# Weight steps of the first MLP by a list of places, and the next batch's attention spread evenly behind them

## The chip, the core and the metric

The kernel runs on one core of a Trainium2 chip. TensorE (PE) multiplies into eight banks of PSUM; VectorE (DVE), ScalarE (ACT) and GpSimd (POOL) compute beside it, and SyncE (SP) issues the DMAs. Each engine works through its own queue in order and waits on semaphores for the others. The metric is the device time of one launch in microseconds. Before the change the median of three runs is 712.6 us (712.22 to 713.0).

## The reference

Four batches of 768 steps pass through three layers, all in float32: a gated linear attention (8 heads of 48), a mixer with a channel MLP, and a gated unit.

```python
state = alpha[:, :, t, :, None] * state + np.einsum('bhd,bhe->bhde', k[:, :, t], v[:, :, t])
y[:, :, t] = np.einsum('bhd,bhde->bhe', q[:, :, t], state)
...
h = xt @ U @ V
u = x + h.transpose(0, 2, 1)
ch = np.maximum(u @ w_ch1, 0.0) @ w_ch2        # 384 -> 1536 -> 384
return (u + ch).astype(np.float32)
...
h = np.maximum(x @ w_in, 0.0)                  # then norm, spatial product, gate, w_out
```

The weights of the MLP arrive as 64-bit floats.

## The kernel before

**Float32 by halves.** A float32 operand is kept as a high part and a rest, and each product is made of three matmuls (`mm3`, `up_group`, lines 259 and 345).

**The weights.** The MLP's weights w_ch1 and w_ch2 come in twelve tiles, W0 to W11 (index `f`), each 128 by 768. Turning one tile from 64-bit words into two parts takes six instructions on three engines: `low_part` on ACT (L211), two integer operations on DVE (L217, L220), an addition on POOL (L223, which needs both), then `split` copies the sum into the high part on ACT (L564) and subtracts for the rest on DVE (L228). `Stage.begin` issues the first four; each call of `Stage.finish(1)` issues one of the last two for the oldest tile begun. So between the addition on POOL and the copy on ACT stands a semaphore: ACT waits in its queue until POOL is done.

**The first MLP.** Batch 0's attention (`first_batch`) runs ahead of everything. Then the MLP of batch 0 runs: up products of nine matmuls into one of two banks ("mm"), ACT takes the positive part (h, L360), DVE its rest (hl, L341), and two groups later nine down products add into three banks. At the end of a run of tiles DVE adds those banks to the block (L411). `FIRST` sets the runs: tiles 0 to 4 for both halves of the sequence side by side (the second half's sums lie in the banks "x" that attention uses otherwise), then runs of tiles, one half after the other.

**What is woven in.** After every three matmuls the MLP calls `pull()`. In batch 0 it begins and finishes weight tiles at the calls listed in `BEGINS` and `ENDS`, and advances batch 1's attention (`attend(1)`) by as many steps as `due()` says. `need(n)` forces a tile's conversion when a group is about to use it. Nothing else sets the order: each engine's queue is the order in which this code issues.

**Attention of batch 1.** Four pairs of heads, numbered 4 to 7. For a pair: two scans on DVE ahead of it (`prepare`, L690 and L702), each followed by a multiplication on POOL (L679); `flip` on PE, taken to SBUF by ACT as kn (L734); `added` on PE; then `state`: ACT writes the decays (L781) into spare columns of one of the two PAIR banks and copies the sums out (L782), and DVE runs six scans (L785) that read the decays there; `keep` on ACT (L795, L796); `scores` on PE into the PAIR banks and their mask on DVE (L756); `inner` and `outer` products on PE (L806, L816) and their `take` on ACT (L831). `mix` steps turn the pair before (L946, L962); they use the bank ALONE.

Of the kernel before, what the change touches and what calls it, by code (L numbers as in the profile page):

```python
# [47 lines left out]
NP = H // 2  # L48
# [4 lines left out]
DS = 8  # L53
NCH = S // CH
# [20 lines left out]
PAIR = PLACES["x"][0:2]  # L75
# [18 lines left out]
def gla_mixer_gating_kernel(ctx: ExitStack, tc: tile.TileContext, akq, v, vT, u, v3, w12, w_in, wsT, b_sp, w_out, out):  # L94
    nc = tc.nc
# [38 lines left out]
    class Stage:  # L134
# [4 lines left out]
        def __init__(self, pool, items, places=(), width=E, most=1):  # L139
            self.narrow = lambda: pool.tile([128, width], U32, name="narrow", tag="narrow", bufs=2)  # L140
            self.items, self.free = list(items), list(places)
            self.loaded, self.late, self.begun, self.most, self.scaled = [], [], 0, most, 0

        def fill(self, most=99):
            while self.items and len(self.loaded) < most:
# [24 lines left out]
            low_part(self.loaded[self.scaled][1])  # L170
            self.scaled += 1

        def begin(self, room=None):
# [6 lines left out]
            place, words, t, n, wide, finish = self.loaded.pop(0)  # L180
            if wide and not place:
                t = (room or self.narrow())[0 : words.shape[0], 0:n]
            if wide and not self.scaled:
                low_part(words)
            self.scaled = max(0, self.scaled - 1)
            x = narrowed(words, t) if wide else words
            self.late.append((self.begun, finish(x), place))
            self.begun += 1
            return True

        def step(self):
# [21 lines left out]
    def narrowed(words, t):  # L213

        words = words.rearrange("p (n w) -> p n w", w=2)
        low, high = words[:, :, 0], words[:, :, 1]
# [3 lines left out]
        nc.vector.scalar_tensor_tensor(  # L220
            out=t, in0=high, scalar=0xC0000000, in1=t, op0=ALU.bitwise_and, op1=ALU.bitwise_or
        )
        nc.gpsimd.tensor_tensor(out=t, in0=t, in1=low, op=ALU.add)  # L223
        return t.bitcast(F32)

# [83 lines left out]
    class ChannelMlp:  # L309
# [54 lines left out]
        def up_both(self, blocks, f):  # L364
            w = self.wts
            wh, wl = w[f][:, 0], w[f][:, 1]
            both = [self.psp.tile([128, 512], F32, name="ps_1", tag="mm") for _ in blocks]

            for ends in (False, True):
                for (t, uh, ul), ps in zip(blocks, both):  # L370
                    parts = [(wh, ul, k) for k in range(KE)] if ends else [(wx, uh, k) for wx in (wh, wl) for k in range(KE)]
                    for i, (wx, ux, k) in enumerate(parts):
                        nc.tensor.matmul(
                            out=ps[:, 0:TB], lhsT=wx[:, k * 128 : (k + 1) * 128], rhs=ux[:, k, :],
                            start=i == 0 and not ends, stop=ends and i == KE - 1,
                        )
# [203 lines left out]
    with ExitStack() as fast:  # L580
# [133 lines left out]
        class Pair:  # L714
# [61 lines left out]

            def state(self, pd):

                decay = pd[:, 0, TB : TB + DS * NCH]
                pe = seen[:, seq[self.n], 1:].rearrange("p (o c) -> p o c", o=1)  # L780
                nc.scalar.activation(out=decay.rearrange("p (e c) -> p e c", c=NCH), in_=pe.to_broadcast([128, DS, NCH]), func=AF.Copy)  # L781
                nc.scalar.activation(out=add.rearrange("p (n x) -> p x n", x=SIDES), in_=pd[:, :, 0 : D * NC], func=AF.Copy)  # L782
                after = apool.tile([128, D, NCH], F32, name="after", tag="after", bufs=1)
                for e in range(0, D, DS):
                    nc.vector.tensor_tensor_scan(  # L785
                        out=after[:, e : e + DS].rearrange("p e c -> p (e c)"), data0=add[:, e * NCH : (e + DS) * NCH], data1=decay,
                        initial=0.0, op0=ALU.add, op1=ALU.mult,
                    )
                self.after = after
# [189 lines left out]
        def attend(b, blocks):  # L979
# [5 lines left out]
            if b * NP not in ready:  # L985
# [6 lines left out]
                yield  # L992
                next(p0)
                yield
            for i in range(NP):
                n = b * NP + i
# [16 lines left out]
                move_some(moves, 3)  # L1013
                yield
                pair.mask(pair.scores())
                next(ahead, None)
                move_some(moves, 3)
                yield
                move_some(moves, 3)
# [6 lines left out]
                yield  # L1026
                if n + 3 < NPAIR:
                    load_pair(n + 3)
                mix = Mix(us, pair.hp, stk) if pair.hp < KE else None
                yield  # L1030
            mix.take(mix.flip(0))
# [37 lines left out]
        def first_batch(blocks):  # L1069
# [27 lines left out]
            for n in range(NP - 1):  # L1097
# [7 lines left out]
                pair.inner(0)  # L1105
                next(ahead)
                if n == 2:
                    weights.scale()
                    weights.scale()
# [17 lines left out]
            weights.begin(narrow[0])  # L1127
            weights.begin(narrow[1])
            weights.scale()
# [9 lines left out]
            flipped(0)  # L1139
            weights.finish(1)  # L1140
            weights.begin()
# [8 lines left out]
            weights.finish(1)  # L1150
            weights.finish(1)
            gp = mixes[0].product()
            weights.finish(1)
            mixes[0].keep(gp)
            flipped(2)
# [4 lines left out]
            summed(1, 0)  # L1160
            gp = mixes[2].product()
            mixes[2].keep(gp)
            for blk in range(NB):
# [3 lines left out]
            for m, blk, engine in (  # L1167
                (0, 0, nc.gpsimd), (0, 1, nc.gpsimd), (1, 0, nc.gpsimd), (2, 0, nc.vector), (1, 1, nc.vector), (2, 1, nc.vector)
            ):
                t, hi, lo = blocks[blk]  # L1170
                rest(lo[:, m, :], t[:, m, :], hi[:, m, :], engine)
            weights.finish(1)
            weights.finish(1)
            yield
            load_pair(5)
# [5 lines left out]
        rest_of_first = first_batch(blocks)  # L1181
        next(rest_of_first)
        nxt = []
        more = attend(1, nxt)
        steps = chain(rest_of_first, more)

        def gating_steps():
            yield from check_alpha()
# [20 lines left out]
        def pull():  # L1209

            nonlocal pulls, done
            pulls += 1
            if b == 0 and pulls in ENDS:
                weights.finish(1)
            if b == 0 and pulls in BEGINS:
                weights.begin()
# [12 lines left out]
        def need(n):  # L1229
            weights.until(N_SMALL + n)  # L1230
# [3 lines left out]
        mlp = ChannelMlp(w12s.parts, hpool, ps, pull, need)  # L1234
        for b in range(B):
            if b == 0:
                n_steps = N_STEPS + 4
# [204 lines left out]
```

## Time and profile before

| what | us |
|---|---|
| median of three runs | 712.6 |
| the profiled execution | 714.88 |
| its span | 712.9 |
| PE busy | 685.0 |
| DVE busy | 342.3 |
| ACT busy | 283.7 |
| POOL busy | 203.1 |

The profiled execution took 714.88 us, of which 712.9 lie between its first and last instruction. Busy times are unions of an engine's instructions; PE's ends are modelled, so its busy time says little about its pace. What an engine waited for, and when, is read from the timeline.

### The profile page before, as it was taken

What the parts mean: (1) busy time and instruction counts of PE and PEld (TensorE: products, weight loads), DVE (VectorE), ACT (ScalarE), POOL (GpSimd) and SP (SyncE); (2) the same over time, 40 slices, a digit from 0 to 9 for tenths busy, and PEclk for the clock granted to TensorE, in tenths of its full rate; (3) what the DMA queues carried; (4) which work ended last, traced back from release to release, by engine and by line L of the source; (5) the groups of instructions that cost most, each with busy time, mean ns of one, the idle gap of its engine ahead of it and who ended that gap; (6) DMA issues with size and microseconds to landing.
All of it is one profiled execution on the core that took longest, in us unless ns stands there. A gap on an engine that the chain in (4) does not pass through costs nothing.

```text
span 712.9 us, 14466 instructions
## 1 busy us (share of the span) xinstructions
PE 685.0 (96%) x6124; PEld 653.9 (92%) x6124; DVE 342.3 (48%) x620; ACT 283.7 (40%) x552; POOL 203.1 (28%) x172
## 2 busy tenths in 40 slices
PE   7988878999999999999999999999999999999996
PEld 6878867899999999999999999989999989999996
DVE  7998987556444335433132784351252143225211
ACT  3874446664454534454331543332231232224111
POOL 5534533215111031110030131343333223333211
PEclk9999999999999999999999999999999999999999
DMA  8699104443543310401004353300011003000001
GB/s 335 194 346 225 28 2 85 78 92 69 114 72 68 81 22 8 111 2 35 2 1 158 103 165 107 122 1 31 5 35 65 34 1 100 9 26 24 11 34 39
DMA packets 21178, 54.20 MB, mean 76 GB/s; under 512 B 2704, under 2 KB 12816, under 8 KB 19824
## 3 DMA queue, kind: packets, MB, share of 16 engines
q1 hardware_dynamic: 21104, 53.18, 27.5%
q8 instruction: 50, 0.82, 0.5%
q14 instruction: 24, 0.20, 0.1%
HBM read 42.55 MB, written 9.44 MB: 73 GB/s over the span
## 4 chain that ended last, share of the span: by engine, by line
PE 82%; DVE 12%; ACT 3%; issue 2%; POOL 1%; DMA 0%; DVEq 0%; ACTq 0%
PE banks L353 19%; PE banks L262 18%; PE banks L264 17%; PE banks L263 17%; PE banks L816 2%; DVE bw L690 2%; DVE narrow L217 1%; DVE fw L702 1%; PE banks L962 1%; PE banks L747 1%; PE banks L806 1%; DVE w L228 1%; PE banks L774 1%; PE banks L731 1%; PE banks L946 1%
## 5 line engine op out<-in xcount | busy, mean ns | idle before, releaser
L353 PE MATMUL banks<-partuh,w 128*128 128x384 f32 x564 | 131.0, 340 | 4.6 <-DVE hl L341 4.6
L353 PEld LDWEIGHTS banks<-partuh,w 128*128 128x128 f32 x564 | 100.4, 189 | 6.2 <-DVE hl L341 5.8
L341 DVE SCALAR_TENSOR_TENSOR hl<-banks,h 128x384 fp32r<-128x384 f32 x96 | 52.9, 552 | 104.0 <-ACT h L360 103.3
L262 PE MATMUL banks<-h,w 128*128 128x384 f32 x288 | 99.9, 347 | 0.9 <-DVE ub L411 0.9
L264 PE MATMUL banks<-hl,w 128*128 128x384 f32 x288 | 96.9, 336 | 0.0
L263 PE MATMUL banks<-h,w 128*128 128x384 f32 x288 | 96.7, 336 | 0.0
L513 DVE TENSOR_TENSOR vsb<-banks,bb 128x384 f32<-128x384 f32 x32 | 17.8, 558 | 129.2 <-PE banks L264 129.2
L360 ACT ACTIVATE h<-banks 128x384 fp32r<-128x384 f32 x94 | 45.8, 488 | 73.8 <-PE banks L353 73.2
L228 POOL TENSOR_TENSOR partul<-ub,partuh 128x384 fp32r<-128x384 f32 x45 | 46.1, 1049 | 88.7 <-ACT partuh L297 75.9
L519 ACT ACTIVATE gh<-gt 128x384 fp32r<-128x384 f32 x32 | 16.8, 525 | 126.3 <-DVE gt L516 126.3
L228 POOL TENSOR_TENSOR gl<-gt,gh 128x384 fp32r<-128x384 f32 x32 | 32.5, 1015 | 120.7 <-ACT gh L519 120.7
L263 PE MATMUL banks<-wsph,vl 128*128 128x384 f32 x192 | 65.1, 339 | 1.0 <-POOL vl L228 0.9
L353 PE MATMUL banks<-partul,w 128*128 128x384 f32 x282 | 66.0, 341 | 0.0
L262 PE MATMUL banks<-wsph,vh 128*128 128x384 f32 x192 | 64.9, 338 | 0.0
L264 PE MATMUL banks<-wspl,vh 128*128 128x384 f32 x192 | 64.8, 338 | 0.0
L262 PEld LDWEIGHTS banks<-h,w 128*128 128x128 f32 x288 | 54.4, 189 | 2.7 <-DVE ub L411 1.6
L263 PEld LDWEIGHTS banks<-h,w 128*128 128x128 f32 x288 | 54.5, 189 | 0.0
L264 PEld LDWEIGHTS banks<-hl,w 128*128 128x128 f32 x288 | 54.4, 189 | 0.0
L353 PEld LDWEIGHTS banks<-partul,w 128*128 128x128 f32 x282 | 50.0, 189 | 0.7
L679 POOL TENSOR_TENSOR akq<-akq,bw 128x768 f32<-128x768 f32 (+1 forms) x15 | 24.6, 1640 | 82.4 <-DVE bw L690 82.4
L679 POOL TENSOR_TENSOR akq<-akq,fw 128x768 f32<-128x768 f32 (+1 forms) x15 | 24.9, 1662 | 62.6 <-DVE fw L702 50.9
L228 POOL TENSOR_TENSOR vl<-vt,vh 128x512 fp32r<-128x512 f32 x20 | 27.1, 1379 | 49.8 <-ACT vh L483 49.8
(184 smaller groups left out, 1374.0 us busy)
## 6 DMA issues: line engine op xcount, KB each, us to landing
akq<-in_akq SPq DMA_DIRECT2D x24, 434.4 KB, 7.3
bits<-in_w SPq DMA_DIRECT2D x12, 768.0 KB, 13.3
x2d<-ub SPq DMA_DIRECT2D x8, 576.0 KB, 3.4
ub<-x2d SPq DMA_DIRECT2D x8, 576.0 KB, 5.3
out_y<-ob SPq DMA_DIRECT2D x24, 192.0 KB, 1.9
v<-in_v SPq DMA_DIRECT2D x15, 288.0 KB, 7.7
words<-in_w_in SPq DMA_DIRECT2D x8, 384.0 KB, 3.2
words<-in_wsT SPq DMA_DIRECT2D x4, 576.0 KB, 5.2
```

The lines of the kernel that those rows point to most:

```text
L228: engine.tensor_tensor(out=out, in0=x, in1=hi.bitcast(F32), op=ALU.subtract)
L262: nc.tensor.matmul(out=ps, lhsT=wh, rhs=xh, start=first, stop=False)
L263: nc.tensor.matmul(out=ps, lhsT=wl, rhs=xh, start=False, stop=False)
L264: nc.tensor.matmul(out=ps, lhsT=wh, rhs=xl, start=False, stop=last)
L341: nc.vector.scalar_tensor_tensor(out=hl, in0=ps[:, 0:TB], scalar=0.0, in1=h.bitcast(F32), op0=ALU.max, op1=ALU.subtract)
L353: nc.tensor.matmul(out=ps[:, 0:TB], lhsT=wx[:, k * 128 : (k + 1) * 128], rhs=ux[:, k, :], start=i == 0, stop=i == len(parts) - 1)
L360: nc.scalar.activation(out=h, in_=ps[:, 0:TB], func=AF.Relu)
L513: nc.vector.tensor_tensor(out=vsb, in0=psv[:, 0:TB], in1=self.g["bb"][:, blk * TB : (blk + 1) * TB], op=ALU.add)
L519: nc.scalar.activation(out=hi, in_=gt, func=AF.Copy)
L679: engine.tensor_tensor(out=chunks(x)[:, c], in0=chunks(x)[:, c], in1=chunks(by)[:, c, 1:CW], op=ALU.mult)
L690: nc.vector.tensor_tensor_scan(out=bw[:, ::-1], data0=a[:, 1 : AW + 1][:, ::-1], data1=ends[:, ::-1], initial=0.0, op0=ALU.mult, op1=ALU.max)
L816: nc.tensor.matmul(out=self.py[HW * h : HW * h + D, x, j * CH : (j + 1) * CH], lhsT=self.w[:, c - 1, h, :], rhs=self.q[:, c * CH : (c + 1) ...
```

## The change

`FIRST` gets one more run: tiles 8 and 9, then 10 and 11, each one half after the other, in place of 8 to 11. One list, `FIRST_STEPS`, says at which `pull()` a tile is finished by one step ("f"), begun ("b"), or attention advances by one step ("s"). Attention is otherwise spread evenly from pull 71. `up_both` calls `pull()` once more, so later calls bear a number higher by one. `begin` is cut in `high` and `add`, and the DVE operations now stand ahead of `low_part` on ACT. In `state` the decays go to the bank ALONE, and `mix.flip(1, ALONE)` stands ahead of them. The last part of `prepare` (a check on ACT, L706) moves to the end of a pair. In `first_batch` two of four copies move from DVE to ACT, and two of three rests from POOL to DVE.

```diff
-FIRST = (0, 5, 8, 12)
+FIRST = (0, 5, 8, 10, 12)
-BEGINS = (1, 9, 17, 25, 34, 43, 54, 65, 76, 87)
-AHEAD, N_AHEAD, HELD = 20, 5, 62
-ENDS = tuple(x + y for x in BEGINS for y in (10, 12))
+FIRST_STEPS = {
+    5: "f", 6: "b", 13: "fbf", 22: "fbf", 31: "fbf", 40: "fbf", 49: "fbf", 58: "f", 59: "ss", 67: "ss",
+    76: "fbf", 86: "fbf", 98: "fbf", 110: "fbf", 116: "f", 122: "f",
+}
+AHEAD, N_AHEAD = 71, 4
...
+        def high(self, room=None):
+            place, words, t, n, wide, finish = self.loaded.pop(0)
...
+            self.raised.append((place, words, t, wide, finish, self.scaled > 0))
+            self.scaled = max(0, self.scaled - 1)
+        def add(self):
+            place, words, t, wide, finish, scaled = self.raised.pop(0)
+            if wide and not scaled:
+                low_part(words)
+            x = both_parts(words, t) if wide else words
+            self.late.append((self.begun, finish(x), place))
...
                 hs.append((h, hl))
+                if len(hs) == 1:
+                    self.pull()
...
-                decay = pd[:, 0, TB : TB + DS * NCH]
+                decay = ps.banks[:, ALONE, TB : TB + DS * NCH]
...
+                if mix:
+                    pt = mix.flip(1, ALONE)
                 pair.state(pair.added())
                 if mix:
-                    mix.take(mix.flip(1, ALONE))
+                    mix.take(pt)
...
-            for x in range(NB):
-                pair.take(x, nc.vector)
+            pair.take(0)
+            pair.take(1, nc.vector)
...
-            if b == 0 and pulls in ENDS:
-                weights.finish(1)
-            if b == 0 and pulls in BEGINS:
-                weights.begin()
+            if b == 0:
+                for x in FIRST_STEPS.get(pulls, ""):
+                    if x == "f":
+                        weights.finish(1)
+                    elif x == "b":
+                        weights.begin()
+                    else:
+                        next(steps, None)
...
-            if mlp.held or pulls <= HELD:
-                return min(N_AHEAD, (pulls - AHEAD) // 4)
-            return N_AHEAD + -(-(pulls - HELD) * (n_steps - N_AHEAD) // (groups - HELD))
+            return -(-max(0, pulls - AHEAD) * (n_steps - N_AHEAD) // (groups - AHEAD))
```

The first place is DVE's queue where the side-by-side run ends. The tile W7 is `bits_370`, and its rest is the row `w12_913` before and `w12_924` now; `ub_177` and `ub_178` are the two halves' sums. Before:

```order
L228 TENSOR_TENSOR w12_913<-narrow_873,w12_913 128x768
L341 SCALAR_TENSOR_TENSOR hl_927<-banks_80,h_926 128x384
L411 TENSOR_TENSOR ub_177<-banks_80,ub_177 128x384 x3
L341 SCALAR_TENSOR_TENSOR hl_953<-banks_80,h_952 128x384
L411 TENSOR_TENSOR ub_178<-banks_80,ub_178 128x384 x3
L690 SCALAR_TENSOR_TENSOR bw_123<-akq1_85,ends_101 128x780
L693 RECIPROCAL starts_104<-bw_123 128x12
L217 TENSOR_SCALAR narrow_986<-bits_374 128x768
L220 SCALAR_TENSOR_TENSOR narrow_986<-bits_374,narrow_986 128x768
L228 TENSOR_TENSOR w12_977<-narrow_918,w12_977 128x768
```

Now:

```order
L358 SCALAR_TENSOR_TENSOR hl_909<-banks_80,h_908 128x384
L430 TENSOR_TENSOR ub_177<-banks_80,ub_177 128x384 x3
L708 MEMSET ends_101 128x6
L709 SCALAR_TENSOR_TENSOR bw_123<-akq0_84,ends_101 128x780
L712 RECIPROCAL starts_104<-bw_123 128x12
L358 SCALAR_TENSOR_TENSOR hl_944<-banks_80,h_943 128x384
L430 TENSOR_TENSOR ub_178<-banks_80,ub_178 128x384 x3
L245 TENSOR_TENSOR w12_924<-narrow_877,w12_924 128x768
L721 SCALAR_TENSOR_TENSOR fw_124<-akq0_84,starts_104 128x780
L358 SCALAR_TENSOR_TENSOR hl_972<-banks_80,h_971 128x384
L709 SCALAR_TENSOR_TENSOR bw_123<-akq1_85,ends_101 128x780
```

W7's rest stood ahead of both halves' sums and stands behind them now; pair 4's scans (on `akq0`), which had been run earlier, stand around it.

The second place is ACT's queue where the tile W8 (`bits_372`) and pair 4 (`state` of `after_1021`, now `after_1038`) meet. Before:

```order
L211 ACTIVATE bits_372<-bits_372 128x768
L360 ACTIVATE h_926<-banks_80 128x384
L360 ACTIVATE h_952<-banks_80 128x384
L734 ACTIVATE kn_968<-banks_80 128x384 x2
L564 ACTIVATE w12_977<-narrow_918 128x768
L700 ACTIVATE seen_115<-bw_123 128x12
L211 ACTIVATE bits_374<-bits_374 128x768
L781 ACTIVATE banks_80<-seen_115 128x96
L782 ACTIVATE add_121<-banks_80 128x2x288
L360 ACTIVATE h_1031<-banks_80 128x384
L795 ACTIVATE state_119<-after_1021 64x11x48
L796 ACTIVATE state_119<-after_1021 64x48x11
```

Now:

```order
L377 ACTIVATE h_1006<-banks_80 128x384
L800 ACTIVATE banks_80<-seen_115 128x96
L801 ACTIVATE add_121<-banks_80 128x2x288
L725 ACTIVATE fw_124,over_118<-akq0_84,below_113 128x780
L225 ACTIVATE bits_372<-bits_372 128x768
L583 ACTIVATE w12_1055<-narrow_1050 128x768
L814 ACTIVATE state_119<-after_1038 64x11x48
L815 ACTIVATE state_119<-after_1038 64x48x11
L377 ACTIVATE h_1101<-banks_80 128x384
L850 ACTIVATE y3_1153<-banks_80 48x384 x2
```

The copy of W8 (`w12_977`, now `w12_1055`) stood four instructions behind its low part; it follows it at once now, and pair 4's keep (the two `state` rows) and an h stand behind it.

The third place is ACT's queue between the take of pair 5 (`ub`, the last row of the one batch) and the kn of pair 6. Before:

```order
L706 ACTIVATE fw_124,over_118<-akq2_86,below_113 128x780
L564 ACTIVATE w12_1291<-narrow_1150 128x768
L211 ACTIVATE bits_464<-bits_464 128x768
L831 ACTIVATE ub_771<-banks_80 48x384 x2
L831 ACTIVATE ub_772<-banks_80 48x384 x2
L360 ACTIVATE h_1368<-banks_80 128x384
L734 ACTIVATE kn_1382<-banks_80 128x384 x2
L953 ACTIVATE yb_1394<-banks_80 128x384
```

Now:

```order
L850 ACTIVATE ub_926<-banks_80 48x384 x2
L850 ACTIVATE ub_927<-banks_80 48x384 x2
L725 ACTIVATE fw_124,over_118<-akq2_86,below_113 128x780
L377 ACTIVATE h_1381<-banks_80 128x384
L225 ACTIVATE bits_462<-bits_462 128x768
L583 ACTIVATE w12_1392<-narrow_1387 128x768
L753 ACTIVATE kn_1394<-banks_80 128x384 x2
L972 ACTIVATE yb_1406<-banks_80 128x384
```

Before, the copy of W10 (`w12_1291`) and the low part of W11 stood ahead of pair 5's take; now the low part of W10 (`bits_462`) and at once its copy (`w12_1392`) stand between that take and pair 6's kn.

## Rows read from the trace of the kernel before

**Rows 1.** Windows: us, busy PE, PEld, DVE, ACT, POOL, PEclk, DMA share, GB/s.

```profile
90.00:100.00 10.00, 5.09 (x107) 4.53 (x111) 9.93 (x17) 4.47 (x9) 4.08 (x3) 1.00 0.01 2
...
170.00:700.00 530.00, 528.98 (x4317) 510.88 (x4316) 207.10 (x427) 185.26 (x365) 133.79 (x115) 1.00 0.19 52
```

**Rows 2.** PE's waits over the span: who for whom, total us, times, longest.

```profile
PE banks L747 <- DVE after L785: 5.8, 3, 2.8
PE banks L353 <- DVE hl L341: 4.6, 4, 1.6
PE banks L731 <- issue: 3.1, 3, 2.5
```

**Rows 3.** Timeline of PE, up groups: start, us, instruction, shape, count, idle before.

```profile
54.35 0.79 PE L353 MATMUL banks<-partuh,w 128*128 128x384 f32 x3 [1.57 <-DVE hl L341]
...
57.61 0.68 PE L353 MATMUL banks<-partuh,w 128*128 128x384 f32 x3
...
60.73 0.68 PE L353 MATMUL banks<-partuh,w 128*128 128x384 f32 x3
...
86.39 0.68 PE L353 MATMUL banks<-partuh,w 128*128 128x384 f32 x3
```

**Rows 4.** Timeline of DVE and POOL around 97 us, one weight tile and a pair.

```profile
95.95 0.96 DVE L220 SCALAR_TENSOR_TENSOR narrow<-bits,narrow 128x768 uint32<-128x768 uint32 x1
96.83 0.95 DVE L228 TENSOR_TENSOR w<-narrow,w 128x768 fp32r<-128x768 f32 x1
97.15 2.33 POOL L223 TENSOR_TENSOR narrow<-narrow,bits 128x768 uint32<-128x768 uint32 x1 [1.64 <-DVE narrow L220]
97.70 1.57 DVE L785 TENSOR_TENSOR_SCAN after<-add,banks 128x96 f32<-128x96 f32 x6
99.19 1.93 DVE L702 TENSOR_TENSOR_SCAN fw<-akq,starts 128x780 f32<-128x780 f32 x1
```

**Rows 5.** Timeline of DVE and POOL, single instructions.

```profile
57.24 0.55 DVE L217 TENSOR_SCALAR narrow<-bits 128x768 uint32<-128x768 uint32 x1
...
91.97 1.77 DVE L690 TENSOR_TENSOR_SCAN bw<-akq,ends 128x780 f32<-128x780 f32 x1
...
101.03 0.53 DVE L341 SCALAR_TENSOR_TENSOR hl<-banks,h 128x384 fp32r<-128x384 f32 x1
101.19 1.69 POOL L679 TENSOR_TENSOR akq<-akq,fw 128x768 f32<-128x768 f32 x1 [1.72 <-DVE fw L702]
101.48 1.01 DVE L756 TENSOR_TENSOR sm<-banks,causal 128x384 f32<-128x384 f32 x2
...
114.87 1.48 DVE L411 TENSOR_TENSOR ub<-banks,ub 128x384 f32<-128x384 f32 x3
```

**Rows 6.** Timeline of ACT: what a pair and a weight tile take there.

```profile
92.71 0.87 ACT L734 ACTIVATE kn<-banks 128x384 f32<-128x384 f32 x2 [4.07 <-PE banks L731]
...
95.41 0.73 ACT L782 ACTIVATE add<-banks 128x576 f32<-128x576 f32 x1
...
99.30 1.16 ACT L795 ACTIVATE state<-after 64x528 f32<-64x528 f32 x1 [2.79 <-DVE after L785]
...
102.91 0.94 ACT L706 ACTIVATE fw<-akq,below 128x780 f32<-128x780 f32 x1 [1.28 <-POOL akq L679]
...
106.96 2.02 ACT L831 ACTIVATE y<-banks 48x384 f32<-48x384 f32 x4 [2.25 <-PE banks L816]
109.00 0.84 ACT L564 ACTIVATE w<-narrow 128x768 fp32r<-128x768 f32 x1
109.75 0.90 ACT L211 ACTIVATE bits<-bits 128x768 uint32<-128x768 uint32 x1
```

**Rows 7.** Timeline of PE: a pair's outer products, and batch 1's last flips.

```profile
105.46 1.46 PE L816 MATMUL banks<-akq,state 128*48 128x64 f32 x44
...
159.44 0.82 PE L946 MATMUL banks<-ident,ub 128*128 128x128 f32 x6
```

**Rows 8.** Window behind the gap at 97 us, columns as in Rows 1.

```profile
100.00:104.00 4.00, 4.00 (x36) 3.93 (x28) 2.49 (x4) 2.64 (x4) 1.69 (x1) 0.57 0.02 4
```

More of the change, by code (lines that the diff above doesn't have):

```diff
@@ L141, in __init__ @@
             self.items, self.free = list(items), list(places)
-            self.loaded, self.late, self.begun, self.most, self.scaled = [], [], 0, most, 0
+            self.loaded, self.raised, self.late, self.begun, self.most, self.scaled = [], [], [], 0, most, 0
         def fill(self, most=99):
@@ L171, in scale, with begin @@
             self.scaled += 1
-        def begin(self, room=None):
+        def high(self, room=None):
+            place, words, t, n, wide, finish = self.loaded.pop(0)
+            if wide and not place:
+                t = (room or self.narrow())[0 : words.shape[0], 0:n]
+            if wide:
+                high_part(words, t)
+            self.raised.append((place, words, t, wide, finish, self.scaled > 0))
[6 more added lines that the diff above has]
+            self.late.append((self.begun, finish(x), place))
+            self.begun += 1
+        def begin(self):
             self.fill(1)
@@ L179, in begin @@
                 self.finish()
[L180 to L188, printed above, removed]
+            self.high()
+            self.add()
             return True
@@ L211, in low_part, with high_part @@
         nc.scalar.activation(out=low, in_=low, func=AF.Copy, scale=2.0**-29)
-    def narrowed(words, t):
-        words = words.rearrange("p (n w) -> p n w", w=2)
-        low, high = words[:, :, 0], words[:, :, 1]
+    def high_part(words, t):
+        high = words.rearrange("p (n w) -> p n w", w=2)[:, :, 1]
         nc.vector.tensor_scalar(
@@ L222, in narrowed, with both_parts @@
         )
+    def both_parts(words, t):
+        low = words.rearrange("p (n w) -> p n w", w=2)[:, :, 0]
         nc.gpsimd.tensor_tensor(out=t, in0=t, in1=low, op=ALU.add)
@@ L984, in attend @@
             moves, mix, last = [], None, None
-            if b * NP not in ready:
+            first = b * NP not in ready
+            if first:
                 p0 = prepare(b * NP)
@@ L991, in attend @@
                 yield
-                yield
-                next(p0)
                 yield
@@ L1005, in attend @@
                 yield
+                if mix:
+                    pt = mix.flip(1, ALONE)
                 pair.state(pair.added())
                 if mix:
-                    mix.take(mix.flip(1, ALONE))
+                    mix.take(pt)
+                if first and i == 0:
+                    next(p0)
                 move_some(moves, 3)
@@ L1015, in attend @@
                 pair.mask(pair.scores())
-                next(ahead, None)
                 move_some(moves, 3)
@@ L1028, in attend @@
                     load_pair(n + 3)
+                next(ahead, None)
                 mix = Mix(us, pair.hp, stk) if pair.hp < KE else None
@@ L1107, in first_batch @@
                 if n == 2:
-                    weights.scale()
-                    weights.scale()
+                    low_part(weights.loaded[1][1])
+                    low_part(weights.loaded[2][1])
                 after = FirstPair(n + 1, us, moves, tags)
@@ L1126, in first_batch @@
             narrow = [up.pool.tile([128, KE * TB], U32, name="narrow", tag=x) for x in ("uh0", "ul0")]
-            weights.begin(narrow[0])
-            weights.begin(narrow[1])
-            weights.scale()
+            low_part(weights.loaded[0][1])
+            weights.scaled = N_SMALL + 1
+            weights.high(narrow[0])
+            weights.high(narrow[1])
+            weights.high()
+            for _ in range(N_SMALL + 1):
+                weights.add()
             before()
@@ L1139, in first_batch @@
             flipped(0)
+            weights.high()
             weights.finish(1)
-            weights.begin()
             for x in range(NB):
@@ L1150, in first_batch @@
             weights.finish(1)
+            gp = mixes[0].product()
+            mixes[0].keep(gp)
             weights.finish(1)
-            gp = mixes[0].product()
+            flipped(2)
             weights.finish(1)
-            mixes[0].keep(gp)
-            flipped(2)
             gp = mixes[1].product()
@@ L1162, in first_batch @@
             mixes[2].keep(gp)
+            weights.add()
             for blk in range(NB):
@@ L1166, in first_batch @@
             busy(4, ps.tile([128, 512], F32, "ps_w", "mm"))
-            for m, blk, engine in (
-                (0, 0, nc.gpsimd), (0, 1, nc.gpsimd), (1, 0, nc.gpsimd), (2, 0, nc.vector), (1, 1, nc.vector), (2, 1, nc.vector)
-            ):
+            for blk in range(NB):
                 t, hi, lo = blocks[blk]
-                rest(lo[:, m, :], t[:, m, :], hi[:, m, :], engine)
-            weights.finish(1)
+                for m in range(KE):
+                    rest(lo[:, m, :], t[:, m, :], hi[:, m, :], nc.gpsimd if blk == m == 0 else nc.vector)
             weights.finish(1)
@@ L1183, in gla_mixer_gating_kernel @@
         nxt = []
-        more = attend(1, nxt)
-        steps = chain(rest_of_first, more)
+        steps = chain(rest_of_first, attend(1, nxt))
         def gating_steps():
@@ L1212, in pull @@
             pulls += 1
-            if b == 0 and pulls in ENDS:
-                weights.finish(1)
-            if b == 0 and pulls in BEGINS:
-                weights.begin()
+            if b == 0:
[6 more added lines that the diff above has]
+                        next(steps, None)
             while done < due():
@@ L1236, in gla_mixer_gating_kernel @@
             if b == 0:
-                n_steps = N_STEPS + 4
+                n_steps = N_STEPS + N_AHEAD
             elif b + 1 < B:
```

## The prediction

> **What bounds the kernel now.** I read the windows first, then PE's list of waits, then the timeline of the front on each engine. The windows [rows 1] split the span: from 170 to 700 us PE is busy for 528.98 of 530 us, and the change touches nothing there that PE waits for. So only the front can move. There DVE is the fuller engine: 9.93 of 10 us between 90 and 100, while PE has 5.09. PE's waits [rows 2] name the same: three waits of 5.8 us for the scans of L785 (scores may not enter the PAIR banks before the scans have read the decays there), four waits of 4.6 us for hl, and 3.1 us before flips. The timeline of PE [rows 3] gives the pace without waits: one group of 18 matmuls in 60.73 - 57.61 = 3.12 us, so 0.52 for the three between two pulls. From 54.35 to 86.39 lie nine groups: 32.04 us where nine times 3.12 is 28.1.
>
> **The rule by which queues are added up.** Rows 4 show what the two engines do to each other. POOL's addition is issued at 97.15 and takes 2.33, because DVE's rest (0.95) runs until 97.78; from there it needs 1.70. DVE's scan L702, issued at 99.19, takes 1.93: POOL ends at 99.48, and 1.64 follow. The scans of L785, which read a PSUM bank, run beside POOL at full pace (1.57). So an SBUF-only instruction of DVE and one of POOL exclude each other, and who starts first goes through; hl, mask and L411 read PSUM and are free. The Trainium skill, SBUF — State Buffer, section "Who interferes with whom", says it as a lock on a shared port pair: the first to issue keeps it for its whole instruction. By that rule, and the trace agrees (2.33 against 1.70), a POOL addition that becomes ready as DVE goes from L220 straight to a scan comes after the scan; if the two shared the port instead, each of the first two waits below would be shorter by one scan, 1.77.
>
> **Front, until the second up group (54.35 before).** DVE now does hl ahead of W1's rest (0.95 [rows 4]) and of W2's two operations (0.55 [rows 5] and 0.96), 2.46 less ahead of it; but two block rests come to DVE (estimate 0.55 each, half of 0.95 for half the width and a little), and they exclude POOL's late addition of W1 and its one rest (estimate 0.9 more). 2.46 - 1.1 - 0.9 gives about -0.45: 53.9. No row shows this order; bounds -1.5 (nothing excluded) and +0.6 (POOL's rest comes last).
>
> **Side-by-side run.** Pair 4's scans are gone from here, and a tile comes every nine pulls, 9 x 0.52 = 4.68 us. A tile needs 0.55 + 0.96 + 0.95 on DVE and 1.70 on POOL, exclusive: 4.2 us, and hl can run beside POOL. So no hl is late and PE keeps its pace: 156 matmuls, 27.05 us, to the last six down products of W4's first half at 81.0. Before, that point was 86.39 - 3.12 + 12 x 0.173 = 85.35 (0.173 is 3.12 / 18). So -4.35 with the front; at worst two hl waits stay (+2).
>
> I count from there, from 0, and let each step begin when the one it waits for ends; the passing of a semaphore (under 0.1) is left out. What PE does between two pulls costs 0.52 per three matmuls, a pair's flips 0.82 [rows 7], its added products, scores and inner products about 0.9 each (estimate, from the flips and the outer products, 1.46, of the same rows).
>
> **W7's rest.** DVE's queue is now hl (0.55), first sums (products end at 1.04; 1.15 to 2.6), pair 4's scan (1.77, reciprocal 0.2: 4.65), hl (5.2), second sums (1.48: 6.65), W7's rest: 7.6. PE wants it at 5.2 (1.04 + 6 x 0.52 + 1.04). A new wait of 2.35; even without the scan the second sums cannot start before 4.2, so at least 1.4. Behind it on DVE stands pair 4's second scan.
>
> **Pair 4 (A).** Scan L702 to 9.4; POOL's multiplication 1.69, to 11.1; the scan for pair 5 is excluded until then and ends at 12.75, reciprocal 12.95; ACT notes the decay product, takes an h, writes the decays (0.2 + 0.5 + 0.27, estimates) and copies the sums (0.73 [rows 6]): 14.6; L785 to 16.2; hl; W8's two operations (1.5) to 18.2; scan L702 to 20.0; masks (1.01) to 21.0. PE would be ready for inner products at 17.5: 3.3 of wait by DVE alone. But W8's addition on POOL follows the scan, to 21.7, and the copy of W8, which ACT now has right ahead of pair 4's keep, waits for it: 22.55. Keep is two of 1.16: 24.9. Outer products start there instead of at 18.4: 6.5 lost. Between: 3.3 if POOL goes first and the copy is no hindrance, 7 at most. I take 6.5. The scores no longer wait for L785; that is worth nothing here, since mask and keep are later than they.
>
> **Pair 5 (B).** Outer products 1.46, six down products 1.04: 27.4. L411 1.5, W8's rest 0.95, W9's operations 1.5, the scan of pair 6 with reciprocal 2.0, then POOL 1.70 and the copy 0.84; behind that copy ACT has the decays and copy of pair 5 (1.2): 37.0. Scores wait for it; PE is there at 33.2, so 3.8. L785 1.57, scan 1.77, masks 1.01 follow: 41.4, against 39.5 on PE: 1.4 more. Outer ends at 43.1.
>
> **Pairs 6 and 7 (C, D).** Both now have the low part and the copy of a tile between a take and the next kn: take 2.02, fw 1.1, h 0.5, low 0.90, POOL 1.70, copy 0.84, kn 0.87, yb 0.5, from 43.1 to 51.6; the added products of pair 6 would have come at 48.4: 3.2. Then added 0.9, ACT's 1.1, L785 1.57, keep 2.3, and outer products end near 59.7. The same chain again for pair 7 gives 68.5, where PE is ready at 65.5: 3.0. With its scans, W11's rest and mask, outer ends at 77.6; two and a half groups of pulls later (2.6) the flips at 80.2. Without low part, POOL and copy (3.4 us) neither wait exists; so they lie between 0 and 3.5 each.
>
> **Decays in ALONE.** The next writers of that bank are the mixer's product and the next flip, both behind keep, so nothing new waits: 0, and up to 0.5 each if it did.
>
> **The sum.** 81.0 + 80.2 = 161.2 against 159.44 for the same flips before [rows 7]: +1.8. PE's clock is on top: after the gap at 97 us the granted clock was 0.57 over 4 us [rows 8], the lower level, 1.2 in place of 2.4 GHz, for 3.4 of them, and PE did 1.7 us less. That happened twice before and is in the 159.44. Now A (6.5 idle of 7.4) and one or two of the gaps behind B, C and D should bring it again; but only what lies on the chain counts (outer and down products behind A 1.7, little of the others, which wait for ACT anyway): +2.5, bounds 0 and +6. Together +4.3. After the flips all is as before. The trace's own execution took 714.88, its span 712.9; it lies 2.3 above the median, and the difference is carried to the median: 712.6 + 4.3 = **717**.
>
> **Rivals.**
> 1. *Faster.* The copies do not hold ACT: POOL's additions come a scan earlier, so that keep, decays and kn are not late. For it: L785 no longer holds scores (5.8 us) and the first stage gives 4.35. Against: POOL lost to a DVE instruction already begun [rows 4]. Then A is the 3.3 of the mask, B loses the scan of 2.0 and 1 more (2.2), C and D are 1 each: 3.2 + 3.0 + 2.2 + 2.0 = 10.4 less than forecast, though the lost time of one engine turns up in part behind the next wait: about 707, 705 with the clock up. It decides once POOL ends two microseconds earlier.
> 2. *No change.* The same at half strength: A 5, B 3.8, C and D 2 each: 4.3 less, 712.6.
> 3. *Slower, and more.* The lower clock falls behind all four gaps with its full 1.7 and the front gives nothing: 717 + 0.45 + 4 = 721.5.
> 4. *The freed scores do nothing.* That they lose one wait and meet another (mask, then the copy in ACT) is part of the forecast; were it not so, A alone would be 3 smaller: 714.
>
> **Numbers.** Forecast with rivals 3 and 4, slower: 0.64, its own range 714 to 722. Rival 1: 0.28. Rival 2: 0.08. About 0.2% (1.4 us) is what a measurement tells from no change. The range reaches to rival 1's bound: 705 to 723.
>
> **What would show it.** Right: the up groups of the first ten stand 3.12 apart with no wait for hl; PE waits for W7's rest (DVE w, 2 us); a gap of 6 us before pair 4's outer products, released by ACT's state; ACT's copies of W8 to W11 each with an idle of one to five microseconds released by POOL; scores of pair 5 released by ACT's add. Wrong: if those copies start without idle, or if DVE is idle between 82 and 110 us, the chain is not what I say; if the clock never falls, the 2.5 go. If first-stage groups still wait, the 4.35 go, and it is slower than 717.

## The result, and the profile after

The changed kernel takes 720.79 us, median of four runs (719.2 to 722.59), against 712.8 us (712.22 to 714.3): a ratio of 1.0109, 95% interval 1.0088 to 1.013. It is slower, on the side and inside the range of the forecast, and 3.8 us above its value. The profiled execution took 719.2 us with a span of 717.5 at a mean clock of 0.985; the kernel before had 714.88, 712.9 and 0.994. By the two profiled executions the change costs 4.3 us, by the medians 8.0; the second is the measured result.

The windows of the kernel after, with the columns of [rows 1]: us, busy time of PE, PEld, DVE, ACT and POOL, then PEclk (the granted clock of PE, 1.00 being full speed), DMA share and GB/s.

```profile
40.00:86.00 46.00, 43.88 (x261) 41.64 (x259) 37.97 (x57) 24.42 (x44) 17.62 (x9) 1.00 0.78 199
86.00:170.00 84.00, 69.88 (x1025) 63.55 (x1026) 51.08 (x88) 44.58 (x84) 26.00 (x14) 0.90 0.33 62
170.00:700.00 530.00, 528.98 (x4318) 511.47 (x4317) 209.75 (x435) 187.38 (x369) 134.50 (x117) 1.00 0.19 53
```

The same two stretches of the front in the kernel before:

```profile
40.00:86.00 46.00, 40.16 (x244) 37.91 (x241) 41.83 (x52) 24.93 (x47) 21.01 (x12) 1.00 0.75 200
86.00:170.00 84.00, 73.90 (x1081) 68.23 (x1080) 56.10 (x97) 47.32 (x89) 26.12 (x17) 0.96 0.36 69
```

From 170 us on nothing changed (528.98 us of 530, as in [rows 1]). In the first stretch PE does 3.7 us more than before; from 86 to 170 it does less, and its clock is 0.90. Of two levels, 1.00 and 0.50, that is (1 - 0.90) x 84 / 0.5 = 16.8 us at the lower one, against 6.7 before. PE's waits in the kernel after, between 45 and 175 us (total, times, longest), answer to [rows 2]:

```profile
PE banks L965 <- ACT kn L753: 5.8, 2, 2.9
PE banks L766 <- ACT add L801: 2.3, 1, 2.3
PE banks L825 <- DVE sm L775: 2.2, 2, 2.1
PE banks L370 <- DVE w L245: 2.2, 1, 2.2
PE banks L835 <- ACT state L814: 1.4, 1, 1.4
PE banks L310 <- DVE stk L989: 0.9, 1, 0.9
PE banks L981 <- ACT yb L972: 0.8, 1, 0.8
PE banks L835 <- ACT state L815: 0.7, 1, 0.7
```

The waits for hl and for the scans of the decays are gone, 10.4 us of [rows 2]. In their place PE waits for ACT (kn, add, state) and for DVE (W7's rest, masks). The timeline of PE in the kernel after shows where (start, us, instruction, shape, count, idle before and its releaser); it answers to [rows 3] and [rows 7]:

```profile
52.41 0.80 PE L370 MATMUL banks<-partuh,w 128*128 128x384 f32 x3
...
55.64 0.68 PE L370 MATMUL banks<-partuh,w 128*128 128x384 f32 x3
...
79.56 0.33 PE L279 MATMUL banks<-h,w 128*128 128x384 f32 x1
...
87.09 0.79 PE L370 MATMUL banks<-partuh,w 128*128 128x384 f32 x3 [2.17 <-DVE w L245]
...
101.12 0.31 PE L825 MATMUL banks<-sm,v 64*48 64x64 f32 x2 [2.06 <-DVE sm L775]
...
104.19 0.45 PE L835 MATMUL banks<-akq,state 128*48 128x64 f32 x2 [1.38 <-ACT state L814]
105.31 2.58 PE L835 MATMUL banks<-akq,state 128*48 128x64 f32 x42 [0.67 <-ACT state L815]
...
117.72 0.93 PE L766 MATMUL banks<-akq 64*64 64x64 f32 x48 [2.26 <-ACT add L801]
...
132.04 0.55 PE L965 MATMUL banks<-ident,ub 128*128 128x128 f32 x3 [2.83 <-ACT kn L753]
...
150.93 0.55 PE L965 MATMUL banks<-ident,ub 128*128 128x128 f32 x3 [2.92 <-ACT kn L753]
...
163.36 0.82 PE L965 MATMUL banks<-ident,ub 128*128 128x128 f32 x6
```

The outer products at 105.31 take 2.58 us where they took 1.46 [rows 7]: that is the lower clock. The last flips come at 163.36 instead of 159.44. What holds ACT at pair 4 is seen on the other engines of the kernel after:

```profile
97.96 0.96 DVE L233 SCALAR_TENSOR_TENSOR narrow<-bits,narrow 128x768 uint32<-128x768 uint32 x1
...
98.84 1.78 DVE L721 TENSOR_TENSOR_SCAN fw<-akq,starts 128x780 f32<-128x780 f32 x1
...
99.09 3.15 POOL L240 TENSOR_TENSOR narrow<-narrow,bits 128x768 uint32<-128x768 uint32 x1 [5.06 <-DVE narrow L233]
...
102.28 0.84 ACT L583 ACTIVATE w<-narrow 128x768 fp32r<-128x768 f32 x1 [5.13 <-POOL narrow L240]
103.03 1.11 ACT L814 ACTIVATE state<-after 64x528 f32<-64x528 f32 x1
```

The scan starts 0.25 us ahead of POOL's addition, which then needs 3.15 us; the copy of W8 stands at the head of ACT for 5.13 us, and keep (L814), whose scans were done at 97.0, goes behind it. The copies of W9 to W11 wait 2.75, 1.99 and 2.54 us for POOL too; W9's addition also ran into a scan and took 2.58 us, those of W10 and W11 did not and took 1.82 and 1.83.

### The profile page after: what moved, and what is told of

Read it like the earlier page. It is cut to its first block, busy times and chain, and to the rows that moved or that the text cites. A ratio compares the mean times of both kernels' runs of the same rounds, so it can differ in the third digit from the quotient of the medians.

```text
span 717.5 us, 14460 instructions
## 1 busy us (share of the span) xinstructions
PE 690.4 (96%) x6124; PEld 659.4 (92%) x6124; DVE 337.2 (47%) x626; ACT 284.6 (40%) x554; POOL 201.6 (28%) x170
## 4 chain that ended last, share of the span: by engine, by line
PE 88%; ACT 4%; DVE 3%; POOL 2%; issue 1%; DMA 0%; ACTq 0%; POOLq 0%; DVEq 0%
PE banks L370 20%; PE banks L279 18%; PE banks L280 18%; PE banks L281 18%; PE banks L835 2%; PE banks L981 2%; PE banks L793 1%; PE banks L825 1%; PE banks L766 1%; POOL narrow L240 1%; PE banks L750 1%; PE banks L965 1%; PE banks L927 1%; PE banks L876 1%; PE banks L936 1%
## 5 line engine op out<-in xcount | busy, mean ns | idle before, releaser
L532 DVE TENSOR_TENSOR vsb<-banks,bb 128x384 f32<-128x384 f32 x32 | 17.8, 558 | 129.6 <-PE banks L281 129.6
L538 ACT ACTIVATE gh<-gt 128x384 fp32r<-128x384 f32 x32 | 16.8, 525 | 126.3 <-DVE gt L535 126.3
L245 POOL TENSOR_TENSOR partul<-ub,partuh 128x384 fp32r<-128x384 f32 x43 | 42.9, 1024 | 83.2 <-ACT partuh L314 70.5
L240 POOL TENSOR_TENSOR narrow<-narrow,bits 128x768 uint32<-128x768 uint32 (+2 forms) x14 | 28.9, 2066 | 55.8 <-ACT bits L225 30.6
```

The source lines that it names most:

```text
L245: engine.tensor_tensor(out=out, in0=x, in1=hi.bitcast(F32), op=ALU.subtract)
L532: nc.vector.tensor_tensor(out=vsb, in0=psv[:, 0:TB], in1=self.g["bb"][:, blk * TB : (blk + 1) * TB], op=ALU.add)
L538: nc.scalar.activation(out=hi, in_=gt, func=AF.Copy)
```

## The experiments

The kernel before ran beside each; its medians there were 712.78 to 713.13, so ratios to it can be compared with 1.0109.

**Copies later (e1) and copies early in the kernel before (e4).** The first undoes one part of the change (in FIRST_STEPS): the copies of W8 to W11 come 4, 4, 5 and 6 pulls later, W11's rest 2. The second does that part alone for W9 to W11 (in the pull of the kernel before).

```diff
-    76: "fbf", 86: "fbf", 98: "fbf", 110: "fbf", 116: "f", 122: "f",
+    76: "fb", 80: "f", 86: "fb", 90: "f", 98: "fb", 103: "f", 110: "fb", 116: "f", 118: "f",
```

```diff
-            if b == 0 and pulls in ENDS:
+            if b == 0 and pulls in ENDS and pulls not in (66, 75, 77, 86, 88, 97):
                 weights.finish(1)
             if b == 0 and pulls in BEGINS:
                 weights.begin()
+                if pulls in (65, 76, 87):
+                    weights.finish(2)
```

> The changed kernel (720.8 us), with ACT's copies of W8 to W11 issued 4 to 8 pulls later, behind keep of the pair in hand instead of ahead of keep, of the decays or of kn. Theory 1 (these copies hold ACT while they wait for POOL): PE's waits before pair 4's outer products (1.38 and 0.67), before pair 5's scores (2.26) and before the flips of pairs 6 and 7 (2.83 and 2.92), 10.1 us in all, go; the masks and scans behind them give back 2 to 4 of it; 712 to 715 us. Theory 2 (DVE's denser queue sets the pace, the copies only fill ACT's idle time): the waits stay and change their releaser to DVE; 719 to 721.

> The kernel before (712.8 us) with one part of the change alone: the copies of the last three weight tiles are issued right behind their begin (pulls 65, 76, 87) instead of ten pulls later. Theory 1 (a copy right behind its low part holds ACT for the time that DVE and POOL need, 2 to 5 us, and what stands behind it comes late): three waits more of 1 to 3 us, 716 to 720. Theory 2: no more than 1 us, 712 to 714.

e1: 711.69 us, ratio 0.998 (0.9966 to 0.9994): 9.1 us less than the changed kernel, and a little faster than the kernel before. e4: 720.7 us, ratio 1.0103 (1.0089 to 1.0118): 7.6 us lost by that part alone. Theory 1 holds from both sides, and a little beyond what it expected. PE's waits with the late copies:

```profile
PE banks L825 <- DVE sm L775: 3.9, 4, 2.1
PE banks L370 <- ACT w L583: 3.5, 1, 3.5
PE banks L370 <- DVE w L245: 2.2, 1, 2.2
PE banks L766 <- ACT add L801: 1.5, 1, 1.5
```

The waits for kn and state are gone. The one of 3.5 us is new and mine: W11's copy now stands behind keep and is itself late. In e4 the scores wait longer for the scans of the decays [rows 2], nearly all of it at pair 4, since ACT writes the decays behind the copy, which waits 4.27 us for POOL. PE's wait and that copy in e4:

```profile
PE banks L747 <- DVE after L785: 7.6, 2, 6.3
```

```profile
99.46 0.84 ACT L564 ACTIVATE w<-narrow 128x768 fp32r<-128x768 f32 x1 [4.27 <-POOL narrow L223]
```

Neither 9.1 nor 7.6 us is the price of the waits alone. With fewer gaps in PE's work e1 also has less of the lower clock (PEclk 0.94 from 86 to 170 us against 0.90), and e4 has more of it than the kernel before (0.92 against 0.96).

**W7 earlier (e2).**

```diff
-    58: "f", 59: "ss",
+    58: "f", 59: "fss",
```

> The changed kernel with W7's rest issued one group earlier, ahead of pair 4's first scan on DVE. If the wait of 2.17 us at 87.1 is the queue's order on DVE alone, it goes, and with it the stretch of lower clock behind it (PEclk 0.57 in 88 to 92): 717.5 to 719. If the time only comes back in front of pair 4's masks, since the scan is as late as before: 720 to 721.

718.46 us, ratio 1.0073 (1.0061 to 1.0086): 2.3 us back. The wait for W7's rest is gone; the masks' wait grew from 2.06 to 2.85 us, and the waits for add from 2.26 to 3.45 in two places, so part of it did come back there.

**The clock (e3, e5, e9, e11).** Unread matmuls keep PE at work in the gaps; shown is the place ahead of pair 5's scores in e5, the others are alike.

```diff
+        def filler(n):
+            busy(n, ps.banks[:, PLACES["mm"][ps.taken["mm"] % 2], :])
...
+                if b == 1 and i == 1:
+                    filler(9)
                 pair.mask(pair.scores())
```

> The changed kernel with matmuls of 128x128 that nobody reads set into the gaps of PE: 16 before W7's low part, 17 before pair 4's inner and 11 before its outer products, 18 before pair 5's scores, 22 before the second mixer flip of pairs 6 and 7 (0.115 us each, so no more than the gaps hold). The output is the same. If the lower clock behind the gaps costs what the granted clock says (17 us at the lower level between 86 and 140, against 7 in the kernel before) and PE is what is late there, the clock stays at 1.00 and 2.5 to 5 us come back: 716 to 718. If what runs at the lower clock lies beside waits for ACT and DVE, the waits take its place: 720 to 721.5.

720.14 us, ratio 1.0102 (1.0088 to 1.0117). The clock was 0.999, but this says nothing on its price: each filler took 0.23 to 0.25 us, not 0.115, and the sets overran the gaps. The second try has half of them.

> The changed kernel (720.8 us) with half of the fillers of the run before: each of those 128x128 matmuls stands twice in the trace (32 rows for 16), 0.23 us each, so they overran the gaps by 0.9 to 2 us. Now 8 before W7's low part, 8 before pair 4's inner and 5 before its outer products, 9 before pair 5's scores, 11 before the second mixer flips of pairs 6 and 7, which is 1.2 to 2.5 us for gaps of 1.4 to 2.9. If the lower clock costs time on the chain, the clock is near 1.00 and 2 to 4.5 us come back: 716 to 719. If it lies beside waits for ACT and DVE: 720 to 721.

713.82 us, ratio 1.0006 (0.9997 to 1.0015), 7.0 us less than the changed kernel, beyond what I expected. The window of e5, PE's timeline and the copy of W8 on ACT:

```profile
86.00:170.00 84.00, 79.38 (x1151) 73.37 (x1150) 54.55 (x95) 47.07 (x90) 30.18 (x19) 1.00 0.34 62
```

```profile
97.41 1.95 PE L734 MATMUL banks<-ident 128*128 128x128 f32 x16
...
103.84 1.45 PE L841 MATMUL banks<-akq,state 128*48 128x64 f32 x42 [0.80 <-ACT state L821]
...
158.68 0.82 PE L971 MATMUL banks<-ident,ub 128*128 128x128 f32 x6
```

```profile
100.80 0.85 ACT L586 ACTIVATE w<-narrow 128x768 fp32r<-128x768 f32 x1 [5.14 <-POOL narrow L240]
```

PEclk is 1.00 from 86 to 170, the outer products take 1.45 us, and the last flips come 4.7 us earlier than in the changed kernel. Nothing was done to the copies: those of W8 to W11 wait for POOL 5.14, 2.34, 2.02 and 2.58 us, much as in the changed kernel. The gaps are still there (filled), and what differs is the clock. So e5's 7.0 us and e1's 9.1 count a part of the same loss twice; the change costs 8.0 in all.

> The kernel before (712.8 us) with the same unread matmuls in its gaps: 9 ahead of pair 5's flips (gap 2.48 us), 11 and 6 ahead of the scores of pairs 5 and 6 (2.76 and 1.71). Its two stretches of the lower clock (6.9 us, PE busy for most of them) should go. If the clock is worth on this kernel what it was on the changed one (7.0 us for 17.2 us at the lower level): 709.5 to 711. If the 7 us there came from somewhere else than the clock: 712.5 to 713.5.

712.73 us, ratio 0.9992 (0.9981 to 1.0003), and not telling: my fillers stood one pair too late. Corrected:

> The kernel before with the fillers where its gaps are: in the run before this one they stood one pair too late, so the gaps of 2.48 and 2.76 us stayed open and pair 5's flips were held 2 us. Now 9 ahead of pair 4's flips, 11 ahead of its scores, 7 ahead of pair 5's scores. If the lower clock costs 0.4 us for each us at that level, as on the changed kernel: clock 1.00 in 86 to 130 and 709 to 711. If what runs at that level lies beside DVE, which is full there: 712 to 713.5.

711.89 us, ratio 0.9982 (0.9973 to 0.9991). Its window:

```profile
86.00:170.00 84.00, 79.61 (x1149) 74.14 (x1148) 57.83 (x98) 48.41 (x93) 28.79 (x18) 1.00 0.35 69
```

PEclk is 1.00 here too. Holding the clock is worth 1.2 us in the kernel before (713.12 us beside this run) and 7.0 in the changed one. Runs of the kernel before without fillers agree: six of those beside e1 and e5 had a mean clock of 0.999 on their own and took 712.0 to 712.4 us, where the medians are 713.1 and 713.0. With the clock held in both, the change costs 713.82 - 711.89 = 1.9 us (1.7 by the ratios). No price for a microsecond at the lower level comes out. From the windows of the profiled executions and the medians it would be 1.2 / 6.7 = 0.18 in the kernel before and 7.0 / 16.8 = 0.42 in the changed one. Taken from the profiled executions alone it is the other way round: (714.88 - 711.88) / 6.7 = 0.45 and (719.2 - 714.31) / 16.8 = 0.29.

**The decays (e6, e7).** e6 does that part alone in the kernel before, e7 undoes it in the changed one (the reverse of this diff).

```diff
-                decay = pd[:, 0, TB : TB + DS * NCH]
+                decay = ps.banks[:, ALONE, TB : TB + DS * NCH]
...
+                if mix:
+                    pt = mix.flip(1, ALONE)
                 pair.state(pair.added())
                 if mix:
-                    mix.take(mix.flip(1, ALONE))
+                    mix.take(pt)
```

> The kernel before (712.8 us) with one part of the change alone: the decays stand in the mixer's bank, and the mixer's second flip ahead of the added products. If the three waits of scores for L785 (5.8 us) are a price of the shared bank, they go: 707 to 709. If the masks and keep behind L785 are late anyway, PE waits for them instead and little is won: 711 to 713.

> The changed kernel (720.8 us) with the decays back in the bank of the added products and the mixer's second flip behind those. If the freed scores are worth nothing in the changed order (mask and keep are later than they): 720 to 721.5. If they hide a part of the waits: 723 to 726.

e6: 711.43 us, ratio 0.9973 (0.9962 to 0.9984), 1.6 us won: as expected by the second reading, the masks take over (PE waits 3.4 us for them, 0.4 before). e7: 724.06 us, ratio 1.0148 (1.0127 to 1.0169), 3.3 us lost, where the forecast had said nothing would be; this interval and the changed kernel's (1.0088 to 1.013) just touch. PE's waits in e7:

```profile
PE banks L793 <- ACT kn L753: 6.5, 2, 3.3
PE banks L766 <- DVE after L804: 3.5, 1, 3.5
```

Pair 5's scores wait for the scans for 3.49 us where they waited 2.26 for add, and the added products for kn 6.5 where the flips waited 5.8.

**Tiles spread, and the gaps filled too (e8, e10, e12).** The waits of e1 and e2 say which places to move.

```diff
-    5: "f", 6: "b", 13: "fbf", 22: "fbf", 31: "fbf", 40: "fbf", 49: "fbf", 58: "f", 59: "ss", 67: "ss",
-    76: "fbf", 86: "fbf", 98: "fbf", 110: "fbf", 116: "f", 122: "f",
+    5: "f", 6: "b", 13: "fbf", 22: "fbf", 31: "fbf", 40: "fbf", 49: "fbf", 58: "f", 59: "fss", 67: "ss",
+    74: "b", 80: "f", 81: "b", 86: "f", 90: "f", 98: "fb", 103: "f", 106: "fb", 112: "f", 113: "f",
```

> The changed kernel with W8 to W11 spread: W7's rest ahead of pair 4's first scan; W8 begun ahead of pair 4's decay scans, where DVE is idle for 3 us; W9 and W11 begun while DVE waits for PE's sums; every copy where ACT has nothing waiting behind it. Theory 1 (the copies' wait and the place of the tiles in DVE's queue were the loss): of the waits that the run with late copies left (2.17 for W7, 2.06 and 1.53 for masks, 1.50 for the added sums of pair 7, 3.46 for W11's copy) most go, 704 to 708, faster than both. Rival (what is freed is taken by the next link, scan by scan): 710 to 712, as with the late copies alone.

702.77 us, ratio 0.984 (0.9825 to 0.9855): 18.0 us less than the changed kernel and faster than both. Its last flips come at 147.39. PE's waits left between 45 and 175 us:

```profile
PE banks L766 <- POOL akq L698: 2.2, 1, 2.2
PE banks L825 <- DVE sm L775: 1.3, 2, 1.1
```

> The run with the spread tiles (702.8 us) with 8 fillers ahead of pair 4's scores (gap 2.15 us) and 7 ahead of its inner products (1.13), where the clock still falls (PEclk 0.50 to 0.85 in 96 to 104). By the price of the clock so far (0.4 us for each us at the lower level, some 7 us of them): 699.5 to 701.5. If pair 4's masks and keep, not PE, are what is late there: 702 to 703.

707.16 us, ratio 0.9909 (0.9893 to 0.9926): slower than e8, by the filler itself, which waited for hl to be read from the bank that it was to write. PE's timeline in e10:

```profile
97.08 3.78 PE L731 MATMUL banks<-ident 128*128 128x128 f32 x16 [4.83 <-DVE hl L358]
```

With the filler moved:

> The run with the spread tiles with 8 fillers behind pair 4's decay scans (in front of an up group, one step ahead of its scores) and 8 ahead of its inner products. In the run before this one the first set wrote into a bank that hl was still to be read from, and PE waited 4.83 us for that; here the bank is free. If PE at the lower clock is late there: 699.5 to 701.5. If masks and keep of pair 4 are: 702 to 703.5.

701.57 us, ratio 0.9837 (0.9824 to 0.9851), five runs within 0.4 us. Its window:

```profile
86.00:170.00 84.00, 82.14 (x1246) 75.69 (x1248) 65.72 (x113) 52.22 (x98) 33.33 (x22) 1.00 0.37 73
```

Against e8's 702.77 that is 1.2 us, but the intervals of the two overlap and they did not run side by side. The gain is e8's order of steps; that the clock adds to it stays open. That the order counts apart from the clock is seen by comparing e12 with e5, both at a PEclk of 1.00 from 86 to 170: 713.82 - 701.57 = 12.2 us, far outside their intervals. How much of the 12.2 is the copies, how much W7 and the tiles' places on DVE, no run with the clock held separates.

## Why the prediction was right, and by how much it was off

**The mechanism was right in the main.** The parts that the forecast named are those that the runs found: the copies behind their low part (e1, e4), W7's rest (2.17 us, forecast 2.35), and a lower clock behind the gaps (e5). The chain was counted from the last six down products of W4's first half, 79.56 in the kernel after (79.64 in e5):

| us after that point | forecast, without clock | after | clock held (e5) |
|---|---|---|---|
| PE goes on with W7 | 7.6 | 7.5 | 7.5 |
| inner products of pair 4 | 21.0 | 21.6 | 20.0 |
| its outer products | 24.9 | 25.8 | 24.2 |
| scores of pair 5 | 37.0 | 38.2 | 35.1 |
| pair 6 goes on behind kn | 51.6 | 52.5 | 49.1 |
| pair 7 goes on behind kn | 68.5 | 71.4 | 66.6 |
| last flips | 80.2 | 83.8 | 79.0 |

Following ACT, DVE and POOL instruction by instruction gave every station of the chain within 2.5 us of the run with the clock held. The single gaps were less good: 6.5 for A where 4.3 were measured, 3.8 + 1.4 for B where it was 2.3. A part of this is the lower clock. PE came to pair 4's inner products at 99.06 - 79.56 = 19.5 and to pair 5's scores at 115.46 - 79.56 = 35.9, where the forecast had 17.5 and 33.2. With the clock held it came at 17.8 (97.41 - 79.64, where the fillers begin in e5) and at 32.6, so PE's own work was estimated well; the gaps are then 5.0 for A and 2.4 + 0.9 for B, fillers counted as gap. The rest is that what PE waited for was done 0.7 to 1.9 us sooner than in the sum. A late PE shortens the wait behind it, and a wait that is shorter for this reason gives nothing back.

**One sign of being wrong came true.** "If DVE is idle between 82 and 110 us, the chain is not what I say": it was idle there three times, for 9.5 us in all.

```profile
95.43 1.58 DVE L804 TENSOR_TENSOR_SCAN after<-add,banks 128x96 f32<-128x96 f32 x6 [2.98 <-ACT add L801]
...
105.80 0.56 DVE L358 SCALAR_TENSOR_TENSOR hl<-banks,h 128x384 fp32r<-128x384 f32 x1 [4.28 <-ACT h L377]
...
109.08 1.08 DVE L430 TENSOR_TENSOR ub<-banks,ub 128x384 f32<-128x384 f32 x2 [2.25 <-PE banks L281]
```

The sign did not fit the forecast's own sum, in which DVE waits for ACT's add from 12.95 to 14.6 and has nothing to do between the masks at 21.0 and the next sums at 27.4. The stations held, but DVE, full between 90 and 100 us before [rows 1], is not what is full here: its longest wait, 4.28 us, is for an h that stands on ACT behind the copy of W8 and keep.

**The queue rule held.** POOL's addition began as the scan ran and came out at 3.15 us; alone it takes 1.83 (at 147.79 us in the same trace). The Trainium skill, SBUF — State Buffer, "Who interferes with whom", has the shared ports as an exclusive lock and the order of issue as what decides who blocks. The trace agrees in both directions: in e8 the multiplication of POOL was first, and DVE's operation on the next tile took 2.32 us instead of 0.96.

```profile
92.31 2.08 POOL L698 TENSOR_TENSOR akq<-akq,bw 128x768 f32<-128x768 f32 x1 [1.77 <-DVE bw L709]
...
92.89 2.32 DVE L233 SCALAR_TENSOR_TENSOR narrow<-bits,narrow 128x768 uint32<-128x768 uint32 x1
```

**What was mis-sized.**

- *The clock term*, "+2.5, bounds 0 and +6", is the one that carries the miss. In the profiled execution it was 83.8 - 79.0 = 4.8 us, in the medians 7.0, which is outside its bounds. I priced one stretch (1.7 us) and gave the others 0.8 in all because ACT was waited for there. The last two columns of the table show what each cost. The stretch behind W7's wait, which the sum did not have, made 1.6 us by pair 4's inner products; the one at pair 4, the one priced, another 1.5 by pair 5's scores; the one behind pair 5 0.3; the one behind pair 6 1.4. Behind kn PE is again what is late: at pair 6 ACT's copy of the sums waits 1.36 us for PE in the changed kernel and 0.75 in e5.
- *The step from profile to median.* "The difference is carried to the median" failed. In the profiled executions the change costs 4.3 us, just what was forecast, but that is luck: at the last flips the first stage was 1.4 us better than the sum (79.56 for 81.0), the chain 1.2 (79.0 for 80.2) and the clock 2.3 worse, which nearly cancels. The profile before lies 2.1 above its median and the one after 1.6 below, and these 3.7 are the miss of the medians. Executions of one kernel differ in their clock: e1's twelve go from a span of 708.0 us at 0.997 to 713.5 at 0.985, the changed kernel's four have 0.981 to 0.985, and e5's eleven, at 0.997 to 0.999, lie within 0.9 us. That the difference of the medians is this, run by run, is not shown, since only profiled executions show their stretches; for the kernel before the mean clock does not tell it, as runs at 0.992 took from 712.5 to 714.7 us.
- *The front*: -0.45 forecast; the up group began at 52.41 instead of 54.35, so -1.94. The side-by-side run kept its pace of 3.12 without a wait, as forecast. This 1.5 us more than forecast hid part of the clock's loss in the profiled execution.
- *The decays*: "worth nothing here" was wrong; the freed scores are worth 3.3 us in the changed kernel (e7, lower clock included: PEclk 0.88 from 86 to 170 us against 0.90) and 1.6 in the old one (e6). I compared the scores with masks and keep of pair 4 only; at pair 5 the scans are late enough to matter.

**The rivals.** That the copies do not hold ACT (rival 1) is refuted by e1, and no change (rival 2) by the interval of the ratio; the terms of rival 2 add up to 1.5 + 1.4 + 1.2 + 1.0 = 5.1 us and not to 4.3, which changes nothing here. Rival 3 (the lower clock falls behind all four gaps) is nearest in time (721.5) and half right: with W7's there were stretches behind four of the five gaps, none behind pair 7's, but the front did give its gain.

## What to carry to other kernels

In an in-order queue, an instruction that waits for another engine should stand behind what is already ready: here four copies of 0.84 us, issued 4 to 6 pulls too early, cost 9.1 us with the lower clock behind the gaps they made, and moving the steps of five tiles to where the queues stood idle won 18, or 12 with the clock held in both kernels. When gaps in PE's work are changed, price the clock with fillers in the gaps of both kernels before arguing about the waits. And compare two profiles with the spread of their runs at hand: a profiled execution can lie 2 us off its median on either side.

## What the runs showed of the hardware

- PE's clock fell to the lower level (0.50) 0.6 to 1.3 us after PE had gone on behind gaps of 2.06 us (pair 4's masks), 2.17 (W7), 2.26 (pair 5) and 2.83 (pair 6), but not behind the 2.92 us of pair 7. Three stretches lasted 3.4 us; the one at pair 4, with two more gaps in it (1.38 and 0.67 us), 6.8.
- Holding the clock with unread matmuls gave back 7.0 us in the changed kernel and 1.2 in the one before. What a microsecond at the lower level costs is not settled: 0.42 and 0.18 by the medians, 0.29 and 0.45 by the profiled executions.
- A filler matmul of 128x128 f32 stands twice in the trace, 0.12 us each: 32 rows for 16 of them took 3.84 us in e3.
- DVE's L230, with one input in SBUF, also waited for POOL: it took 0.55 us at 97.38 in the changed kernel, with POOL idle, but 1.44 at 64.64 with an addition under way, and 1.40 in e8 with a multiplication under way.
